# Sketched attention and a feed-forward block in one kernel: key-value matrices through DRAM instead of TensorE, and a new order of the work

## The chip, the cores and the metric

The kernel runs on one core of a Trainium2 chip. Five engines work side by side, each through its own list of instructions in order: TensorE (PE) multiplies matrices into PSUM, VectorE (DVE), ScalarE (ACT) and GpSimd (POOL) do the rest, and SyncE (SP) mostly issues transfers. Transfers can also be issued by ACT. Engines wait for each other through semaphores. The metric is the time of one execution on the device, in microseconds.

## The reference

Inputs are q, k and v of shape (4 batches, 4 heads, 1088 tokens, 32), two sketch matrices S1 and S2 of 8 x 32, and for the second block g_ln (128), w_ch1 (128 x 512) and w_ch2 (512 x 128). q, k and v are 32-bit floats; the sketches and weights arrive as 64-bit floats.

```
phi(x):   a = x @ S1.T ; b = x @ S2.T ; outer product of a and b, 64 numbers per token
kv  = sum over tokens of phi(k) (64) times v (32)
z   = sum over tokens of phi(k)
att = (phi(q) @ kv) / (phi(q) . z + 1e-6)
x   = att with the four heads side by side: (4, 1088, 128)
xn  = (x - mean) / sqrt(var + 1e-6) * g_ln
out = x + relu(xn @ w_ch1) @ w_ch2
```

## The kernel before

**Staging.** Each of the four batches has 1088 tokens. They are worked on in 9 groups u of 128 tokens (the last is a remainder). For the second block the tokens are cut into ten chunks c: chunks 0 to 7 are halves of a batch's first 1024 tokens (4 tiles of 128 each), chunks 8 and 9 hold the remainders of two batches each (one tile). All of PSUM is eight banks of 128 x 512 numbers, named A, B, C, D, M, N, O and K; the first four together are `X`, and K is also `KV`, in whose columns the key-value matrix and some small sums live.

**The order of the work** is written out in full. Every step is a small function marked `@op`; the text `PROGRAM` (L910 to L1000) lists their calls in order, with letters for the engine (V, A, G, S for DVE, ACT, POOL, SP) or the bank. Each engine runs its own steps in the order of that text. Waits follow from the data.

**The weights** (`w_ex` to `w_mul`, L275 to L342) come as 64-bit words and are turned to 32-bit floats by shifts and masks on DVE, ACT and POOL. The sketches take the same way and end in `s_heads` (L345); `sk` (L373) turns them on PE, and `sk_8`, `sk_q`, `sk_d` and others spread them into the matrices with which keys and queries are multiplied. `fold` (L359) works the mean and g_ln into the first layer's weights. `fill` and `bump` (L241 to L250) are matmuls on ones whose results nobody uses. `c_act` (L183) is a first activation; the table of functions is loaded ahead of it.

**Keys of a batch.** `turn_g` and `turn_r` (L432 to L452) turn the loaded keys on DVE, `k_feat` (L502) makes a and b on PE, `k_tok` (L514) turns them back on DVE, `k_prod` (L520) forms the 64 products, mostly on POOL. `k_sum`, `k_zs`, `k_sc` and `k_sccp` make z and merge it into the query's sketch. `k_val` (L557) sums products times values on PE into columns 0 to 63 of `KV`, each head in its own 32 partitions. Values come by `ld_v` and `ld_vr`; those of batch 0 by one load and `v_flip` and `v_cp`.

**The key-value matrix** must then stand in `kvr` turned, and spread so that each group of 32 partitions holds all heads. In the kernel before this takes three steps: `k_vcp` (L568, ACT) copies it four times side by side to `kvc`, `k_spr` (L573, PE) turns two 128 x 128 blocks into columns 256 to 511 of `KV`, `k_rcp` (L578, ACT) copies them to `kvr`.

**Queries of a batch.** `turn_h` turns them, `q_feat` (L625) makes a, b and the share of the denominator, `q_tok` (L637) turns them back, `q_ac`, `q_den`, `q_rec`, `q_a2` make the division, `q_prod` (L669) the 64 products, `q_turn` (L676) turns these on DVE. `num` (L728) multiplies them on PE with `kvr`: 32 tiles of 32 x 32, each as two matmuls, in 16 places of the array. `num_cp` and `num_r` copy the result to `xT` and `xTr`. The first 512 tokens of batch 0 go another way (`q_dir`, `q_flip`, `num0`).

**Second block.** `hid` (L841) and `relu` (L847) make one of four quarters j of the hidden layer of a chunk, `sec` (L856) the second layer of one tile of 128 tokens. The rows of x, with tokens on partitions, are wanted for the statistics (`st_bn`, `st_ag` on DVE, `st_pow` on POOL) and for the last sum. Chunks in `through_dram` (L774) get them by `row_turn` (L795, DVE), `row_wr` (L800, a write to DRAM) and four reads `row_rd` (L806); the others, here 0, 8 and 9, by `row_pe` and `row_cp` (L785 to L792), turned by PE and copied. The last sum is `fin` (L870, DVE, tile by tile) or `fin_a` and `fin_g` (L876 to L888, ACT then POOL, the whole chunk); `store` and `store_r` write out a quarter or a remainder.

```
    def k_spr(b):
        for i in range(2):
            pe.transpose(KV[:, 256 + P * i : 256 + P * (i + 1)], kvc[:, P * i : P * (i + 1)], ident)
```

Of the kernel before, what the change touches and what calls it, by code (L numbers as in the profile page):

```python
# [24 lines left out]
def kernel(  # L25
# [49 lines left out]
    def copy(eng, o, i):  # L75
        if eng == "A":
            act.copy(o, i)
# [493 lines left out]

    @op
    def k_spr(b):  # L573
        for i in range(2):
            pe.transpose(KV[:, 256 + P * i : 256 + P * (i + 1)], kvc[:, P * i : P * (i + 1)], ident)
# [460 lines left out]
```

## Time and profile before

| what | value |
|---|---|
| three runs | 104.55, 103.06, 103.91 us; median 103.91 |
| the profiled execution | 102.81 us |
| its span, first to last instruction | 100.9 us |
| mean granted PE clock | 0.998 |
| PE, DVE, POOL, ACT busy | 95.3, 74.0, 58.4, 41.3 us |
| transfers issued by SP, by ACT (calls in PROGRAM) | 81, 27 |

A profile is of one execution; its own time is that of the table's second row, and the span leaves out some time around it. In rows of groups, the numbers behind the bar are the busy time in all and the mean in ns of one, and behind a second bar how long the engine stood idle before, and for whom. Rows of the chain and of the timeline begin with the start and the length in microseconds. "PEld" are weight loads of PE, which run beside its matmuls. "SPq" and "ACTq" are the queues in which these engines issue transfers. A line number can be that of a helper: L77, L79 and L82 are the copy and the product that many steps use.

### The profile page before, as it was taken

The numbers are of one execution on the slowest core, as the hardware profiler recorded it, in microseconds if no ns is written. First come the engines' busy times: TensorE is split into PE (matmuls) and PEld (weight loads), VectorE is DVE, ScalarE is ACT, GpSimd is POOL, SyncE is SP. The second block draws the span as 40 slices with busy tenths as digits, with TensorE's granted clock in tenths as the row PEclk, the third lists the DMA queues.
The fourth block names the chain that finished last, engine by engine and source line by source line (L and its number), as shares of the span: only waits on it lengthen the run. The fifth ranks groups of instructions, "written<-read, shape, count | busy, mean of one in ns | idle before, by whom it ended". The sixth has DMA issues, their size and how long they took to land.

```text
span 100.9 us, 3433 instructions
## 1 busy us (share of the span) xinstructions
PE 95.3 (94%) x1355; PEld 68.7 (68%) x1355; DVE 74.0 (73%) x239; ACT 41.3 (41%) x119; POOL 58.4 (58%) x83
## 2 busy tenths in 40 slices
PE   5988999999999999999999999999999999999960
PEld 5765668656656779656588669854469758959950
DVE  2878989789999599699089549999559079661630
ACT  2863754979700720755513353029640030253000
POOL 7115998999588926912999189809920540057000
PEclk9999999999999999999999999999999999999999
DMA  2989999893008760030023220346146445054242
GB/s 76 272 293 389 353 370 275 272 218 88 3 6 301 212 164 3 6 130 0 6 107 106 47 59 0 109 153 187 55 107 204 143 122 148 1 115 132 77 119 64
DMA packets 12367, 13.85 MB, mean 137 GB/s; under 512 B 2880, under 2 KB 8768, under 8 KB 12352
## 3 DMA queue, kind: packets, MB, share of 16 engines
q1 hardware_dynamic: 9968, 11.67, 38.8%
...
## 4 chain that ended last, share of the span: by engine, by line
PE 78%; DMA 5%; POOL 5%; DVE 2%; ACT 2%; SPq 2%; issue 1%; ACTq 0%; POOLq 0%
PE bankO L859 8%; PE bankM L859 8%; DMA w_raw<-in_moe_w_ch_dram 5%; PE bankN L843 5%; PE bankK L560 5%; PE bankC L843 4%; PE bankK L843 4%; PE bankK L859 4%; PE bankB L843 3%; PE bankA L843 3%; PE bankD L843 3%; PE bankM L250 3%; PE bankA L859 3%; PE bankN L859 3%; POOL ob L888 2%; PE bankA L735 2%
## 5 line engine op out<-in xcount | busy, mean ns | idle before, releaser
L82 POOL TENSOR_TENSOR kp<-kf 128x1024 f32<-128x1024 f32 (+4 forms) x9 | 15.9, 1779 | 0.1
L827 POOL TENSOR_SCALAR va<-mv 128x4 f32<-128x4 f32 (+1 forms) x10 | 2.3, 228 | 18.2 <-DVE mv L822 17.7
L82 POOL TENSOR_TENSOR qp<-a,fq 128x1280 f32<-128x1280 f32 (+1 forms) x5 | 11.1, 2219 | 0.2
L859 PEld LDWEIGHTS bankO<-w,hT 128*128 128x128 f32 x80 | 9.7, 192 | 1.9 <-issue 1.9
L829 POOL TENSOR_TENSOR rstd<-va,mhalf 128x4 f32<-128x4 f32 (+1 forms) x10 | 10.3, 1034 | 0.8
L859 PE MATMUL bankO<-w,hT 128*128 128x128 f32 x80 | 10.4, 277 | 0.0
L859 PEld LDWEIGHTS bankM<-w,hT 128*128 128x128 f32 x72 | 9.0, 192 | 1.9 <-issue 1.9
L677 DVE STREAM_TRANSPOSE qpT<-qp 128x1280 f32<-128x1280 f32 (+1 forms) x7 | 9.6, 1365 | 0.0
L250 PE MATMUL bankM<-ones 128*128 128x256 f32 (+1 forms) x28 | 8.3, 440 | 1.2 <-DVE top L180 1.2
L859 PE MATMUL bankM<-w,hT 128*128 128x128 f32 x72 | 9.3, 275 | 0.0
L816 DVE BATCH_NORM_STATS2 st<-x 128x6 f32<-128x128 f32 x32 | 6.7, 272 | 2.5 <-issue 2.5
L250 PEld LDWEIGHTS bankM<-ones 128*128 128x128 f32 x28 | 5.7, 241 | 2.5 <-DVE top L180 1.2
L851 ACT ACTIVATE hT<-bankC 128x512 f32<-128x512 f32 (+1 forms) x6 | 3.3, 551 | 8.3 <-PE bankB L859 4.7
L843 PE MATMUL bankC<-xT,w 128*128 128x512 f32 x12 | 6.1, 592 | 0.0
L843 PE MATMUL bankN<-xT,w 128*128 128x512 f32 (+1 forms) x14 | 6.1, 516 | 0.0
L851 ACT ACTIVATE hT<-bankN 128x256 f32<-128x256 f32 (+1 forms) x6 | 3.0, 498 | 7.2 <-PE bankN L843 7.2
L82 POOL TENSOR_TENSOR a<-fq,rden 128x160 f32<-128x160 f32 (+1 forms) x6 | 2.8, 463 | 5.2 <-DVE rden L659 4.8
L560 PEld LDWEIGHTS bankK<-kp,vn 128*32 128x32 f32 x288 | 4.2, 110 | 2.3 <-issue 1.1
L851 ACT ACTIVATE hT<-bankK 128x512 f32<-128x512 f32 (+1 forms) x6 | 3.1, 522 | 6.2 <-PE bankK L843 5.3
L457 DVE STREAM_TRANSPOSE qT<-qn 128x512 f32<-128x512 f32 x8 | 5.5, 687 | 0.0
L843 PE MATMUL bankK<-xT,w 128*128 128x512 f32 (+1 forms) x12 | 5.4, 530 | 0.0
L735 PE MATMUL bankD<-qpT,kvr 32*32 32x288 f32 (+1 forms) x64 | 5.2, 386 | 0.0
...
## 6 DMA issues: line engine op xcount, KB each, us to landing
...
xd<-xh SPq DMA_DIRECT2D x5, 256.0 KB, 2.6
x<-xd SPq DMA_DIRECT2D x20, 64.0 KB, 2.0
out_dram<-ob SPq DMA_DIRECT2D x19, 64.0 KB, 1.7
out_dram<-ob ACTq DMA_DIRECT2D x13, 64.0 KB, 1.9
w_raw<-in_moe_w_ch_dram SPq DMA_DIRECT2D x2, 256.0 KB, 4.0
```

Source lines behind the costliest of these rows:

```text
L82: by[eng].tensor_tensor(out=o, in0=a, in1=b, op=ALU.mult)
L250: pe.matmul(M[0][:, 0:w], ones[:, 0:P], ones[:, 0:w], start=True, stop=True)
L457: dve.transpose(_ap(dst[b % 2], 0, P, P * 4 * half, [[32, 4], [P, 4], [1, 32]]), src[b][:, 512 * half : 512 * half + 512],)
L560: pe.matmul(KV[D * h : D * h + D, 0:F], vn[b][:, TW * h + D * u : TW * h + D * (u + 1)], kp[:, H * F * u + F * h : H * F * u + F * (h + 1) ...
L677: dve.transpose(_ap(qpT, 0, P, 32 * u0, [[32, u1 - u0], [TW, 8], [1, 32]]), qp[:, H * F * u0 : H * F * u1])
L735: pe.matmul(X[r][D * h : D * h + D, o : o + w], kvr[b % 2][rows, DM * f + D * h : DM * f + D * h + D], qpT[rows, c : c + w], start=(f == 0 ...
L816: dve.bn_stats(out=sts[slot(c)][:, 6 * t : 6 * t + 6], in_=row_ap(c, t))
L827: pool.tensor_scalar(out=vas[slot(c)][:, 0:n], in0=_ap(mvs[slot(c)], 0, P, 1, [[2, n]]), scalar1=1e-6, scalar2=None, op0=ALU.add)
L829: pool.tensor_tensor(out=rstds[slot(c)][:, 0:n], in0=vas[slot(c)][:, 0:n], in1=mhalf[:, 0:n], op=ALU.pow)
L843: pe.matmul(banks[z][:, 0:n], w1[:, P * j : P * (j + 1)], cols(c)[:, a : a + n], start=True, stop=True)
L851: act.activation(o, i, AF.Relu)
L859: pe.matmul(banks[z][:, DM * t : DM * (t + 1)], h[:, 512 * j + P * t : 512 * j + P * (t + 1)], w2[:, DM * j : DM * (j + 1)], start=(j == 0 ...
```

## The change

The turned and spread `kvr` is no longer made by PE and ACT. DVE turns the 64 columns of `KV` in blocks of 32 into `kvt` (`kv_turn`), one transfer writes `kvt` to DRAM (`kv_wr`), four reads put it into each group of 32 partitions of `kvr` (`kv_rd`). The layout of `kvr` is now by head, and `num` reads it so; its two inner loops change places. All ten chunks take their rows through DRAM, so `row_pe` and `row_cp` are not called any more. The whole `PROGRAM` is in another order, with other engines for some steps; SP issues 136 transfers and ACT 7. There are 17 instead of 14 `fill` matmuls. Of the new order the diff shows the start up to the numerator of the first tokens of batch 0, the stretch around `num 1`, and the tail from `row_wr S 4` on.

```diff
--- before.py
+++ after.py
@@ -478,7 +478,8 @@
     kf = const([P, NU * KW], F32, "kf", 2)
     kp = const([P, NU * H * F], F32, "kp")
     zT = const([P, HR], F32, "zT")
-    kvc = const([P, 2 * P], F32, "kvc")
+    kvt = const([P, F], F32, "kvt", 2)
+    kvx = [dram.tile([P, F], F32, name=f"xdk{i}") for i in range(B)]
     kvr = const([P, 2 * DM], F32, "kvr", 2)
 
     @op
@@ -565,20 +566,19 @@
                 )
 
     @op
-    def k_vcp(eng, b):
-        copy(eng, _ap(kvc, 0, P, 0, [[P, 2], [32, 4], [1, 32]]),
-             _ap(KV, 0, P, 0, [[32, 2], [0, 4], [1, 32]]))
-
-    @op
-    def k_spr(b):
-        for i in range(2):
-            pe.transpose(KV[:, 256 + P * i : 256 + P * (i + 1)], kvc[:, P * i : P * (i + 1)], ident)
-
-    @op
-    def k_rcp(eng, b):
-        copy(eng, kvr[b % 2], KV[:, 256:512])
-
-
+    def kv_turn(b):
+        dve.transpose(kvt[b % 2], KV[:, 0:F])
+
+    @op
+    def kv_wr(eng, b):
+        by[eng].dma_start(out=bass.AP(kvx[b].tensor, kvx[b].offset, [[F, P], [1, F]]), in_=kvt[b % 2])
+
+    @op
+    def kv_rd(eng, b, r):
+        by[eng].dma_start(
+            out=_ap(kvr[b % 2], 32 * r, 32, 0, [[F, H], [1, F]]),
+            in_=bass.AP(kvx[b].tensor, kvx[b].offset, [[F, 32], [32 * F, H], [1, F]]),
+        )
 
     QW = H * 32
     W0 = H * 3 * R
@@ -728,13 +728,13 @@
     def num(b, u0, u1):
         w = 32 * (u1 - u0)
         for f in range(2):
-            for r in range(4):
-                for h in range(H):
+            for h in range(H):
+                for r in range(4):
                     rows, o = slice(32 * r, 32 * r + 32), 32 * u0
                     c = TW * (2 * h + f) + 32 * u0
                     pe.matmul(
                         X[r][D * h : D * h + D, o : o + w],
-                        kvr[b % 2][rows, DM * f + D * h : DM * f + D * h + D],
+                        kvr[b % 2][rows, F * h + D * f : F * h + D * f + D],
                         qpT[rows, c : c + w],
                         start=(f == 0), stop=(f == 1), tile_position=(32 * r, D * h),
                     )
@@ -771,7 +771,7 @@
     rstds = const([P, 4], F32, "rstd", 3)
     hT = const([P, JC * 512], F32, "hT", 2)
     obs = const([P, 512], F32, "ob", 4)
-    through_dram = set((1, 2, 3, 4, 5, 6, 7, ))
+    through_dram = set((0, 1, 2, 3, 4, 5, 6, 7, 8, 9))
 
     def rows_of(c):
         return x[c % 4] if c < 8 else x[c - 4]
@@ -908,96 +908,99 @@
 
 
     PROGRAM = """
-    ld_w S 1 2 4; c_ones; ld_g A; c_small; c_ac 0; ld_s A 0; ld_s S 1; c_vpad 0; c_kvb; c_vpad 1;
-    fill 1 128; ld S k 0 0 16; c_act; c_pads 1; c_pads 0; fill 4 256; c_iota; ld S k 0 16 34;
-    c_ac 1; c_m2; c_ident; ld_w S 1 0 2; c_m32; c_m8; ld S k 1 0 34; ld S q 0 16 34;
-    w_low A 1 256 512; w_ex V 0 0 32; w_bits V 0 0 32; w_bits V 1 256 512; w_exf A 0 0 32;
-    ld_h S q 0 0; w_mant V 1 256 512; w_mant A 0 0 32; w_ex V 1 256 512; ld S v 0 0 32;
-    w_e2 V 0 0 32; w_addlow V 0 0 32; w_exf A 1 256 512; w_e3 V 0 0 32; turn_g k 0 0 2;
-    ld_vr S 0 1; s_heads G; fill 1 128; w_e2 A 1 256 512; fill 1 128; c_cg V; ld_vr S 0 0; bump 12;
-    turn_g k 0 2 4; ld_w S 2 0 4; sk; bump 24; sk_8 A; w_e3 V 1 256 512; sk_q; turn_r k 0;
-    ...
+    ld_w S 1 0 2; c_ones; c_small; c_vpad 0; ld_s S 0; fill 1 256; c_act; ld_s A 1; c_ac 0;
+    c_pads 0; c_pads 1; ld S k 0 16 34; c_vpad 1; c_rest; ld S k 0 0 16; fill 1 256; c_ac 1;
+    ld_w S 1 2 4; c_iota; c_ident; ld_vr S 0 0; fill 1 256; w_bits V 0 0 32; c_m8; ld_g S;
+    w_mant A 0 0 32; w_ex V 1 0 256; ld_h S q 0 0; w_ex V 0 0 32; w_bits V 1 0 256; w_exf A 0 0 32;
+    fill 1 256; w_addlow V 0 0 32; ld S q 0 16 34; c_m2; w_e2 A 0 0 32; w_exf V 1 0 256;
+    ld S k 1 0 34; w_e2 A 1 0 256; w_e3 V 0 0 32; turn_g k 0 2 4; ld S v 0 0 32; s_heads G;
+    fill 1 256; fill 1 256; turn_r k 0; w_mant V 1 0 256; w_low A 1 0 256; w_e3 V 1 0 256; sk;
+    ld S k 2 0 34; turn_g k 0 0 2; bump 24; sk_8 A; w_add V 1 0 256; k_feat 0 0 9; ld_vr S 0 1;
+    w_low A 1 256 512; w_ex V 1 256 512; c_m32; w_exf V 1 256 512; ld S q 1 0 34; sk_b;
+    w_bits V 1 256 512; bump 12; k_tok 0 0 0 9; ld_w S 2 0 4; sk_2 A; fill 1 128; k_tok 0 1 0 9;
+    fill 1 256; w_e2 A 1 256 512; turn_h q 0 0; k_prod G 0 6 9; k_sum 0; fill 1 128; k_zs 0;
+    fill 1 128; turn_r q 0; turn_h q 0 1; k_sc 0; fill 4 256; sk_q; w_mant A 1 256 512; k_sccp V 0;
+    k_prod G 0 5 6; sk_d; k_sccp F 0; w_e3 V 1 256 512; c_kvb; sk_qq 0; turn_g k 1 0 4;
+    k_prod G 0 3 5; q_feat 0 4 9; q_dir 0 4 N; k_prod G 0 0 3; q_tok 0 2 4 9; q_tok 0 0 4 9;
+    q_tok 0 3 4 9; q_tok 0 1 4 9; v_flip 0 O; q_cp A 0 4 N 16 24; v_flip 1 K; turn_r k 1;
+    fill 1 128; c_cg V; q_ac G 0 4 9; q_ac0 0 4 N 0; v_cp A 0 O; v_flip 2 D; fill 1 128;
+    v_cp A 1 K; q_den 0 0 4; v_flip 3 M; w_add G 1 256 512; v_cp A 2 D; k_feat 1 0 9; q_den 0 4 9;
+    q_rec 0 0 4; v_cp A 3 M; q_rec 0 4 9; w_mul G 1 0 256; q_b0 0 4 N 0; k_val 0; k_tok 1 0 0 9;
+    c_vpad 3; q_prod0 2 4 N 0; w_mul G 1 256 512; fold D 0 256; kv_turn 0; sk_qq 2; k_tok 1 1 0 9;
+    q_a2 G 0 4 9; kv_wr S 0; f_vcp A; q_flip 2 4 0 A; q_prod0 0 2 N 0; q_flip 2 4 1 O;
+    q_prod G 0 4 9; ld_v S 1 2; k_sum 1; q_flcp A 2 4 1 O; f_spr C; ld_v S 1 3; turn_r q 1;
+    fold M 256 512; q_flcp A 2 4 0 A; k_zs 1; turn_h q 1 1; f_rcp A C; ld_vr S 1 1; q_flip 0 2 0 A;
+    q_flip 0 2 1 M; kv_rd S 0 3; turn_h q 1 0; q_flcp A 0 2 0 A; k_sc 1; num0 2 4 O;
+    ...
+    q_a2 G 1 0 4; k_val 1; num_cp A 0 2 4 8; num_cp V 0 0 4 8; relu A M 0 2 0 2; num_cp V 0 3 4 8;
+    num_cp A 0 1 4 8; row_turn 0; relu A N 0 3 0 2; w_e2 A 2 0 512; hid C 1 3 0 4; w_add V 2 0 512;
+    row_wr S 0; ld_vr S 2 0; k_zs 2; turn_r k 3; hid D 1 2 0 4; ld_v S 2 1; num_r A 0;
+    relu A O 0 1 0 2; w_e3 V 2 0 512; relu A C 1 3 0 4; hid O 1 1 0 4; kv_turn 1; relu A D 1 2 0 4;
+    w_mul G 2 0 512; q_den 1 4 9; kv_wr S 1; turn_g k 3 0 4; hid M 1 0 0 4; ld S q 3 0 34;
+    ld_v S 2 0; q_rec 1 4 9; k_sc 2; k_feat 3 0 9; turn_h q 2 0; relu A M 1 0 0 4; q_a2 G 1 4 9;
+    relu A O 1 1 0 4; c_vpad 2; turn_r q 2; sec M 0 0; q_prod G 1 4 9; turn_h q 2 1; kv_rd S 1 2;
+    ld_v S 2 2; row_turn 1; sec M 0 2; kv_rd S 1 1; k_tok 3 1 0 9; kv_rd S 1 3; k_tok 3 0 0 9;
+    sec N 1 2; ld_vr S 2 1; k_sccp V 2; q_prod V 1 0 4; ld_vr S 3 1; k_prod G 2 0 5; q_feat 2 0 9;
+    kv_rd S 1 0; row_wr S 1; k_sum 3; q_tok 2 3 0 9; ld_v S 2 3; sec N 1 0; q_tok 2 0 0 9;
+    ld_v S 3 1; q_turn 4 9; sec M 0 3; row_rd S 0 1; ld_vr S 3 0; sec N 1 1; k_prod G 2 5 9;
+    q_tok 2 2 0 9; row_rd S 1 2; q_tok 2 1 0 9; sec M 0 1; row_rd S 1 3; k_zs 3; q_turn 0 4;
+    row_rd S 1 0; sec N 1 3; row_rd S 1 1; q_ac G 2 4 9; q_ac V 2 0 4; k_sc 3; q_den 2 0 4;
+    num 1 0 9; q_den 2 4 9; q_rec 2 0 4; q_rec 2 4 9; k_val 2; num_cp A 1 1 0 4; num_cp V 1 3 4 8;
+    num_cp A 1 2 0 4; num_cp V 1 0 0 4; num_cp A 1 1 4 8; num_cp A 1 2 4 8; num_cp V 1 0 4 8;
+    num_cp A 1 3 0 4; row_turn 2; hid B 3 3 0 4; k_prod G 3 0 5; turn_h q 3 1; row_wr S 2;
+    ...
+    sec K 3 0; q_prod V 3 0 4; row_wr S 4; kv_rd S 3 3; hid M 8 2 0 1; row_rd S 8 2; hid A 4 3 0 4;
+    relu V M 8 2 0 1; row_rd S 3 0; st_bn 2; row_rd S 8 0; hid M 8 3 0 1; relu A A 4 3 0 4;
+    hid C 8 0 0 1; q_a2 V 3 4 9; row_rd S 3 3; hid N 4 1 0 4; row_turn 5; relu A C 8 0 0 1;
+    relu A M 8 3 0 1; kv_rd S 3 0; st_ag 2; sec M 8 0; store S 0 3 0 4; relu V N 4 1 0 4; st_pow 2;
+    row_rd S 4 2; q_turn 0 4; hid C 4 2 0 4; row_rd S 4 0; kv_rd S 3 1; q_prod G 3 4 9; fin_a O 2;
+    hid D 5 3 0 4; store S 0 0 0 4; st_bn 3; kv_rd S 3 2; hid B 5 0 0 4; store S 1 1 0 4;
+    relu A D 5 3 0 4; row_rd S 8 1; hid O 4 0 0 4; store S 0 2 0 4; relu A B 5 0 0 4; q_turn 4 9;
+    row_rd S 4 3; relu A C 4 2 0 4; hid D 5 2 0 4; row_wr S 5; relu A O 4 0 0 4; row_rd S 8 3;
+    hid N 5 1 0 4; relu A D 5 2 0 4; store S 1 0 0 4; st_ag 3; st_pow 3; sec M 4 3;
+    relu A N 5 1 0 4; num 3 0 9; fin_g G 2; fin_a K 3; row_rd S 5 3; store S 1 2 0 4; row_rd S 5 2;
+    fin_g G 3; sec M 5 1; store S 1 3 0 4; num_cp A 3 0 4 8; num_cp V 3 1 0 4; num_cp V 3 2 4 8;
+    store S 2 3 0 4; num_cp A 3 1 4 8; num_cp V 3 3 4 8; num_cp A 3 2 0 4; st_bn 8; sec K 5 2;
+    store S 0 1 0 4; num_cp A 3 3 0 4; num_cp A 3 0 0 4; st_ag 8; row_turn 7; num_r A 3;
+    row_rd S 5 1; st_pow 8; hid O 7 2 0 4; row_rd S 4 1; row_turn 6; store S 2 1 0 4; row_turn 9;
+    fin M 8 0; sec K 4 0; row_wr S 7; store S 2 2 0 4; sec B 5 0; store S 2 0 0 4; row_wr S 9;
+    st_bn 4; sec B 5 3; row_wr S 6; store S 3 1 0 4; st_ag 4; sec B 4 1; row_rd S 7 0; st_pow 4;
+    row_rd S 5 0; hid N 9 1 0 1; row_rd S 7 2; hid A 9 0 0 1; hid M 9 2 0 1; store S 3 2 0 4;
+    hid D 7 3 0 4; fin K 4 0; row_rd S 6 1; store_r S 8 0; hid C 7 0 0 4; relu A D 7 3 0 4;
+    row_rd S 7 1; relu A O 7 2 0 4; store_r S 8 1; hid D 7 1 0 4; row_rd S 9 3; sec B 4 2;
+    row_rd S 9 0; relu A D 7 1 0 4; row_rd S 7 3; relu A C 7 0 0 4; hid K 9 3 0 1; row_rd S 6 0;
+    fin B 4 2; hid D 6 1 0 4; st_bn 5; row_rd S 6 3; hid C 6 0 0 4; fin M 4 3; relu A D 6 1 0 4;
+    fin B 4 1; store S 4 1 0 4; hid D 6 2 0 4; relu V C 6 0 0 4; row_rd S 9 1; row_rd S 6 2;
+    st_ag 5; hid O 6 3 0 4; st_bn 7; row_rd S 9 2; st_pow 5; store S 3 0 0 4; sec C 7 3;
+    relu A O 6 3 0 4; relu A D 6 2 0 4; sec N 7 2; fin K 5 2; fin M 5 1; fin B 5 3; fin B 5 0;
+    sec O 7 1; st_ag 7; store S 5 2 0 4; st_bn 9; st_pow 7; st_bn 6; store S 3 3 0 4; sec N 6 1;
+    store S 5 3 0 4; st_ag 6; store S 5 1 0 4; sec B 6 0; st_pow 6; store S 4 0 0 4;
+    store S 4 2 0 4; sec C 7 0; relu V A 9 0 0 1; store S 4 3 0 4; fin O 7 1; fin N 7 2; sec A 6 3;
+    fin C 7 3; fin C 7 0; relu V K 9 3 0 1; store S 7 2 0 4; store A 7 1 0 4; sec C 6 2; fin N 6 1;
+    relu A M 9 2 0 1; st_ag 9; store S 5 0 0 4; fin B 6 0; relu A N 9 1 0 1; store A 7 0 0 4;
+    st_pow 9; fin A 6 3; store A 7 3 0 4; sec D 9 0; fin C 6 2; store S 6 3 0 4; store A 6 2 0 4;
+    fill 1 256; store A 6 1 0 4; store S 6 0 0 4; fin D 9 0; store_r A 9 1; store_r S 9 0;
     """
```

More of the change, by code (lines that the diff above doesn't have):

```diff
@@ new lines @@
+    hid B 2 0 0 4; kv_turn 2; relu A O 2 2 0 4; kv_wr S 2; num_r A 1; row_rd S 0 0; q_a2 G 2 4 9;
+    hid O 2 1 0 4; row_turn 8; q_a2 G 2 0 4; ld_v S 3 3; q_prod G 2 0 4; ld_v S 3 2; hid D 2 3 0 4;
+    relu A O 2 1 0 4; relu A B 2 0 0 4; kv_rd S 2 2; hid O 3 0 0 4; relu V D 2 3 0 4; ld_v S 3 0;
+    kv_rd S 2 1; hid B 3 1 0 4; q_prod G 2 4 9; q_turn 0 4; relu A O 3 0 0 4; kv_rd S 2 0;
+    row_rd S 2 2; sec O 2 2; relu A B 3 1 0 4; row_wr S 8; row_turn 3; kv_rd S 2 3; hid D 3 2 0 4;
+    st_bn 1; row_rd S 2 3; sk_qq 3; sec O 2 3; row_rd S 2 1; k_sccp V 3; relu A D 3 2 0 4; st_ag 1;
@@ new lines @@
+    st_bn 0; st_pow 1; q_feat 3 0 9; row_rd S 2 0; row_wr S 3; sec O 2 0; q_tok 3 0 0 9;
+    k_prod G 3 5 9; fin_a N 1; q_tok 3 3 0 9; sec K 3 1; q_tok 3 1 0 9; q_tok 3 2 0 9; sec K 3 3;
+    st_ag 0; q_ac V 3 4 9; st_pow 0; q_turn 4 9; hid N 8 1 0 1; k_val 3; fin_g G 1; fin_a M 0;
+    q_ac V 3 0 4; num 2 0 9; kv_turn 3; q_den 3 4 9; kv_wr S 3; q_den 3 0 4; row_rd S 3 2;
+    q_rec 3 0 4; sec K 3 2; num_cp A 2 0 0 4; num_cp V 2 3 0 4; num_cp A 2 2 0 4; q_a2 G 3 0 4;
+    num_cp V 2 3 4 8; row_rd S 3 1; num_cp A 2 0 4 8; num_cp A 2 1 0 4; q_rec 3 4 9; fin_g G 0;
```

93 lines of the change are left out of this document (11 added, 82 removed).

## The prediction

> **What bounds the kernel now.** I read the page's totals first, then the chain that ended last, then a table by stage cut at the points where TensorE (PE) starts the query features and the numerators of a batch.
>
> ```profile
> span 100.9 us, 3433 instructions
> ...
> PE 95.3 (94%) x1355; PEld 68.7 (68%) x1355; DVE 74.0 (73%) x239; ACT 41.3 (41%) x119; POOL 58.4 (58%) x83
> ...
> PE 78%; DMA 5%; POOL 5%; DVE 2%; ACT 2%; SPq 2%; issue 1%; ACTq 0%; POOLq 0%
> ```
>
> ```profile
> 12.13:21.16 9.03, 8.92 (x218) 5.78 (x225) 8.20 (x25) 5.75 (x20) 8.35 (x9) 1.00 0.99 297
> 21.16:33.82 12.66, 12.66 (x184) 8.45 (x191) 11.49 (x31) 7.13 (x20) 10.63 (x12) 1.00 0.45 125
> 33.82:58.96 25.14, 25.14 (x500) 18.31 (x508) 19.64 (x50) 9.64 (x29) 16.16 (x14) 1.00 0.26 75
> 72.12:97.40 25.28, 25.12 (x226) 20.18 (x225) 14.18 (x64) 5.41 (x14) 7.57 (x12) 1.00 0.40 110
> 97.40:100.90 3.50, 0.00 (x0) 0.00 (x0) 0.35 (x1) 0.00 (x0) 0.00 (x0) 0.92 0.37 94
> ```
>
> The columns after the stretch are its length and the busy time of PE, weight loads, DVE, ACT and POOL, then clock and DMA. From 21.16 to 97.40 PE has hardly a gap, so these 76.24 us are a queue of matmuls one behind the other. Ahead of it lies a start in which PE waits for data, behind it a tail of 3.50. So three things are to be priced: PE work removed, the start, and whether the new order leaves PE waiting.
>
> **PE work removed.** The chain gives what a group of PE instructions holds the engine.
>
> ```profile
> 20.20 0.58 PE bankO L715 x4
> 20.79 0.37 PE bankK L575 x2
> ...
> 23.78 0.44 PE bankO L787 x4
> ...
> 60.49 0.37 PE bankK L575 x2
> ...
> 75.87 0.11 PE bankN L787
> ...
> 88.53 0.86 PE bankD L843 x2
> ...
> 95.57 0.89 PE bankK L859 x8
> ```
>
> L575 is the spreading transpose, 0.37 in each of four batches (first and last shown); three of them come after 21.16: 1.11. L787 turns the rows of chunk 0 (0.44) and, one tile each, of chunks 8 and 9 (0.11, the last shown): 0.66. Hidden and second layers (0.86 and 0.89 for a whole step) are the same in number. After 21.16, then, 1.77 us of PE work goes. The list has 17 fills for 14; those that come after q_feat 0 cost 0.2 each for 128 columns and are in the start's sum below, and the one behind the last second-layer step has nothing waiting for it: 0.
>
> **Numerators.** The loops over h and r change places; the same 64 matmuls stay.
>
> ```profile
> 40.63 0.38 PE bankA L735 x4
> ...
> 42.16 1.09 PE bankO L859 x8
> ```
>
> ```profile
> 40.56 0.45 PE L735 MATMUL bankA<-qpT,kvr 32*32 32x288 f32 x4
> ...
> 40.82 0.42 PE L735 MATMUL bankA<-qpT,kvr 32*32 32x288 f32 x4
> ...
> 41.06 0.65 PE L735 MATMUL bankA<-qpT,kvr 32*32 32x288 f32 x5
> 41.31 0.47 PE L735 MATMUL bankB<-qpT,kvr 32*32 32x288 f32 x4
> ```
>
> One numerator takes 42.16 - 40.63 = 1.53. In its first half the sixteen tiles follow each other in steps of 0.25 (40.56, 40.82, 41.06); in the second half bank A starts at 41.06 and bank B only at 41.31: where a tile gets its second weights, the queue stands. The new order meets the same tile first, so I take 0. Bounds: 0.45 lost or regained in each of four numerators, -1.8 to +1.8 (at most the whole excess of 1.53 over four steps and a bit, and as much the other way).
>
> **ACT, DVE and POOL.** ACT loses eight copies, the row copies and 20 of 27 DMA issues; DVE gains four turns of 64 columns, row turns of chunks 0, 8 and 9, and some weight decoding.
>
> ```profile
> L77 ACT COPY kvc<-bankK 128x256 f32<-128x256 f32 x4 | 1.5, 373 | 3.2 <-PE bankK L560 2.0 <-PE bankK L531 1.3
> L452 DVE STREAM_TRANSPOSE kT<-kn 128x64 f32<-128x64 f32 x4 | 0.9, 219 | 0.0
> L797 DVE STREAM_TRANSPOSE xh<-xT 128x512 f32<-128x512 f32 x7 | 4.7, 688 | 0.2
> L677 DVE STREAM_TRANSPOSE qpT<-qp 128x1280 f32<-128x1280 f32 x4 | 5.9, 1475 | 0.0
> L677 DVE STREAM_TRANSPOSE qpT<-qp 128x1024 f32<-128x1024 f32 x3 | 3.7, 1218 | 0.0
> L82 DVE TENSOR_TENSOR qp<-a,fq 128x1024 f32<-128x1024 f32 x1 | 1.2, 1224 | 0.0
> L457 DVE STREAM_TRANSPOSE qT<-qn 128x512 f32<-128x512 f32 x8 | 5.5, 687 | 0.0
> L639 DVE STREAM_TRANSPOSE fq<-bankD 128x288 f32<-128x288 f32 x3 | 1.4, 456 | 0.4 <-PE bankD L629 0.4
> ```
>
> kv_turn has the size of L452: 4 x 0.22 = 0.9; the row turns are 0.69 + 2 x about 0.2. These lie beside matmuls, as DVE is busy 19.64 of 25.14 in the middle. They cost PE nothing while DVE is in time, so I laid the three engines' new lists side by side, each instruction with the duration of its own shape. The tightest place is num 1. PE comes to it from the start of k_feat 3 (33.6 by my walk) over that step, eight second-layer steps of 0.89, a query-feature step of about 0.7 and half a microsecond of sums: 42.5. DVE, free at 33.3, has two half turns (1.4), row_turn 1 (0.69), two key and four query turns out of PSUM (8 columns groups, about 2.5 by pitch), q_prod (1.22), q_turn twice (1.48 + 1.22) and small ones (0.7): about 9.2, so 42.5 too. No margin: whatever DVE runs late there, PE waits. At num 2 I find 0.4 of margin, at k_val 3 0.3, at num 3 1.5. I charge 0 and keep 1.5 (half a microsecond at each of the first three) as the bad end.
>
> **The new DRAM way of the key-value matrix.** kv_turn, then a write, then four reads, in place of copy, transpose, copy.
>
> ```profile
> xd<-xh SPq DMA_DIRECT2D x5, 256.0 KB, 2.6
> x<-xd SPq DMA_DIRECT2D x20, 64.0 KB, 2.0
> ```
>
> ```profile
> L808 SPq DMA_DIRECT2D x<-xd x20: 303/423/511, 32.0 to 84.2; - x20
> ...
> 17.30 3.52 SPq L121 DMA_DIRECT2D vn<-in_v_dram  x7
> ```
>
> 0.2 + 2.6 + four issues of 0.43 + 2.0 is 6.5 us from k_val to num if SP is free. The new list puts some twelve microseconds of PE work between k_val 1 and num 1 (eight second-layer steps, four hidden ones), and as much before num 2 and num 3: the way is covered, cost 0. If the cover were gone, a num would wait up to 6.5.
>
> SP is in order, and a read that waits for its write holds all behind it. Behind kv_rd of batch 0 stand the last values of batch 1; behind kv_wr 2 a row read of chunk 0; behind row_wr 5 the row reads and stores of the tail. SP issues 136 transfers instead of 81. At 0.43 each, the 51 from row_wr 4 to the last read of chunk 6 take 22 us and in my walk run from 62.0 to 87.3 with their waits; st_bn 6 wants that read at 90.4, and it lands at 89.0: 1.4 us of slack. So cost 0 here, with a rival below.
>
> The Trainium skill (DMA: Bandwidth & Descriptors, "Issuing engines are not separate DMA queues") holds that issuing from several engines only saves sequencer time, usually small beside the transfer. By it the move to SP costs nothing, as in my sum. The row above gives 0.43 per issue, and 51 of them fill most of that stretch, so here I do not call it small.
>
> **The start.** It changes in order most.
>
> ```profile
> 1.17 0.60 ACTq L104 DMA_DIRECT2D s_raw<-in_S_dram  x1
> 1.80 1.28 ACT L184 ACT_TABLE_LOAD   x1 [1.80 <-issue]
> ```
>
> ```profile
> 3.72 0.17 DVE L277 TENSOR_SCALAR ex<-s_raw 16x32 uint32<-16x32 uint32 x1 [0.38 <-DMA s_raw<-in_S_dram]
> ...
> 7.83 0.29 DVE L277 TENSOR_SCALAR ex<-w_raw 128x256 uint32<-128x256 uint32 x1 [0.90 <-DMA w_raw<-in_moe_w_ch_dram]
> ```
>
> c_act now stands ahead of ld_s on ACT: 0.7 + 1.28 and a short activation put the issue at 2.2 instead of 1.17, so S lands near 4.7 instead of 3.7, and DVE's third instruction waits for it with all masks and decoding behind it. Against that the wait of 0.90 at 7.83 goes, since the first half of w1 is now loaded first. Step by step k_feat 0 comes at 8.5 (7.08 before), and q_feat 0 at 13.3 (12.13): 1.2 late. From there PE has less to do before q_feat 1: the spread (0.37) goes, half of num0 (0.58, L715) is put behind q_feat 1, and some 1.2 of waits of the old order are filled, while two fills between the value flips add about 1.0. That gives q_feat 1 at 21.3, against 21.16. Bounds: 20.5 (S not late, masks ahead) and 23.2 (nothing regained).
>
> **Sum.** 21.3 + 76.24 + 0.58 (the moved half) - 1.77 = 96.3 for the end of PE, 97.40 before. The tail keeps its 3.50: a last sum on DVE, a store. Span 99.8, 1.1 less. The profiled execution took 102.81, so 101.7; its own time lies under the lowest of the three runs (103.06), and against their median of 103.91 the same step gives **102.8**, or 1.1% faster. About 2% is what a measurement of this kernel can tell from no change: below 101.83 or above 105.99.
>
> **Rivals.**
> *The numerators regain their stop.* For it: the stop is seen at every numerator and the loop order is what changes. Against: the first tile met is the same. Worth 1.8: 101.0.
>
> *SP becomes the bound of the tail (slower).*
>
> ```profile
> SPq L808 <- DMA xd<-xh: 5.7, 3, 2.7
> ```
>
> After 58 us the old SP waited 5.7 for written rows, my walk has 1.7; and seven value loads at 17.30 took 0.50 each. With 0.07 x 51 = 3.6 from the issues and half of the missing waits, 2.0, less the 1.4 of slack, PE ends 4.2 later: 107.0. It decides once the last read of chunk 6 lands 1.4 later than 89.0. Against it: ACT's 20 issues and their waits are gone, and DMA share there is 0.40.
>
> *A late start stays late*, or DVE makes PE wait at num 1 and num 2 so that the removed work is only exchanged for waits: 1.9 or 1.5 above the forecast, 104.5. For it speaks the margin of nothing; against it that DVE idles about 1.7 in front of relu D 2 3 and can catch up.
>
> *PE cools in the start.*
>
> ```profile
> 1.17 4.43 PE L250 MATMUL bankM<-ones 128*128 128x128 f32 x14 [1.17 <-DVE top L180]
> ...
> 9.26 1.06 PE bankM L250 x4
> ```
>
> The first 1408 columns of fills took 4.43, but 512 warm ones 1.06, so 2.9 for as many: the first ones run slower by 1.5. In the new order fills end near 5.7 and PE stands 1.4 before sk and 0.8 before k_feat 0. If that makes it slow again, another 1.5: 104.3. The Trainium skill (TensorE: Matmul & The Clock Gate, "Part 1: The HAM clock gate") has the clock halve after an idle window of about 3.4 us, longer than these pauses; by that rule the rival fails, so it gets little.
>
> **Chances.** Forecast 0.47 (its own range 101.8 to 103.9), numerators 0.22, SP 0.15, late start or DVE 0.11, cooling 0.05. The range: 100.9 to 105.9 leaves out part of the numerators' case and most of SP's. Faster by over 2%: 0.22 and a low edge of the forecast, 0.25; slower by over 2%: SP's 0.15 and a little of the late start, 0.17; between, 0.58.
>
> **What would show it.** k_feat 0 near 8.5 and q_feat 1 near 21.3; no PE idle after it but for some tenths at num 1; num still 1.53; k_val to num with kvr in time; PE end near 96.3 and the tail 3.5. The prediction is wrong if q_feat 1 is off by over a microsecond, if num changes its length, or if SP's row reads are what DVE's st_bn waits for.

## The result, and the profile after

The kernel after takes 104.02 us as the median of 22 runs (103.73 to 104.81). The kernel before, run between them, has 104.26 (102.78 to 105.20). The runs of before lie around 103.0 and around 104.6, and the comparison leaves out most of the upper ones as disturbed (by the two medians alone after would be 0.2% faster): the ratio is **1.0087, interval 1.0066 to 1.0108: 0.9% slower**, within the 2%. The forecast was 102.8, 1.1% faster.

The page of the kernel after, its totals and the shares of the chain that ended last:

```profile
PE 97.7 (95%) x1347; PEld 68.6 (67%) x1347; DVE 72.3 (70%) x237; ACT 39.8 (39%) x118; POOL 58.1 (56%) x82
...
PE 61%; SPq 14%; DMA 9%; DVE 7%; issue 3%; POOL 1%; ACT 1%; DVEq 0%; POOLq 0%
```

PE is still the engine that is always busy, but 14% of the chain now is SP's queue, which had 2%. The table by stage, cut as before at the query features of batches 0 and 1, the key features of batch 3, and the last numerators (columns as in the prediction):

```profile
13.12:22.24 9.12, 9.12 (x203) 5.87 (x203) 7.13 (x24) 3.60 (x12) 9.04 (x11) 1.00 0.37 120
22.24:34.47 12.23, 12.23 (x234) 7.08 (x233) 11.03 (x27) 7.19 (x22) 5.52 (x7) 1.00 0.55 172
...
74.32:99.30 24.98, 24.78 (x218) 19.37 (x218) 13.15 (x62) 6.71 (x20) 9.46 (x15) 1.00 0.51 136
99.30:103.00 3.70, 0.42 (x2) 0.01 (x1) 0.35 (x1) 0.00 (x0) 0.00 (x0) 0.83 0.42 109
```

PE has hardly a gap behind 22.24 here either. So the question is when PE gets there, and what the queue of matmuls behind it costs. The starts below are those of the first matmul in the timeline, and the end is that of the last second-layer matmul; the chain's times, which the prediction used, are up to 0.1 later. e3 to e7 are experiments, told in the next section.

| start on PE, us | before | forecast | after | e3 | e1 | e5 | e7 |
|---|---|---|---|---|---|---|---|
| k_feat 0 | 7.09 | 8.5 | 8.05 | 8.15 | 8.16 | 8.15 | 7.89 |
| q_feat 0 | 12.06 | 13.3 | 13.12 | 13.22 | 13.23 | 12.65 | 12.39 |
| q_feat 1 | 21.09 | 21.3 | 22.24 | 22.34 | 21.08 | 20.52 | 20.26 |
| num 1 | 40.56 | 42.5 | 43.84 | 43.94 | 42.69 | 42.13 | 41.82 |
| end of the last second layer | 97.36 | 96.3 | 99.28 | 98.53 | 97.44 | 96.73 | 96.41 |
| q_feat 1 to that end | 76.27 | 75.0 | 77.05 | 76.20 | 76.36 | 76.21 | 76.16 |
| span | 100.9 | 99.8 | 103.0 | 102.2 | 101.1 | 100.4 | 100.1 |

Three things are to be told apart: q_feat 1 comes 0.9 later than forecast; from there to the end PE needs 76.2 to 77.1 where 75.0 was forecast; and the profiled execution of after, the slowest of its 22, needs 0.9 more for that than e3, whose profiled execution (104.01) stands at the median of after. In that tail SP stands in the chain (start, length, piece), and the next fence has the wait of DVE that follows:

```profile
78.45 2.19 SPq L808
...
92.35 0.46 SPq L808
...
94.11 1.16 PE bankB L859 x8
```

```profile
92.15 0.87 DVE L816 BATCH_NORM_STATS2 st<-x 128x6 f32<-128x128 f32 x4 [2.54 <-DMA x<-xd]
```

SP's row reads come late: the last of chunk 6 goes out at 92.35, where the walk of the forecast was done at 87.3. The statistics of chunk 7, whose last read goes out at about 90, let DVE wait 2.54; PE's step at 94.11 waits for DVE, and the 34 second-layer steps behind q_feat 1 take 0.8 more in all, from start to start, than in e3.

### The profile page after: what moved, and what is told of

Its sections match the earlier page's. It is cut to its first block, busy times and chain, and to the rows that moved or that the text cites. A ratio compares the mean times of both kernels' runs of the same rounds, so it can differ in the third digit from the quotient of the medians.

```text
span 103.0 us, 3456 instructions
## 1 busy us (share of the span) xinstructions
PE 97.7 (95%) x1347; PEld 68.6 (67%) x1347; DVE 72.3 (70%) x237; ACT 39.8 (39%) x118; POOL 58.1 (56%) x82
## 4 chain that ended last, share of the span: by engine, by line
PE 61%; SPq 14%; DMA 9%; DVE 7%; issue 3%; POOL 1%; ACT 1%; DVEq 0%; POOLq 0%
SPq L808 9%; PE bankO L843 5%; PE bankK L561 4%; DMA x<-xd 4%; PE bankM L250 4%; PE bankO L859 4%; PE bankM L859 4%; PE bankK L859 4%; PE bankN L859 4%; SPq L893 4%; PE bankB L843 3%; PE bankD L843 3%; DMA s_raw<-in_S_dram 2%; PE bankA L507 2%; DMA xd<-xh 2%
## 5 line engine op out<-in xcount | busy, mean ns | idle before, releaser
L250 PE MATMUL bankM<-ones 128*128 128x256 f32 (+1 forms) x34 | 10.5, 453 | 1.2 <-DVE top L180 1.2
L843 PE MATMUL bankD<-xT,w 128*128 128x512 f32 x18 | 9.4, 604 | 0.0
L250 PEld LDWEIGHTS bankM<-ones 128*128 128x128 f32 x34 | 7.3, 240 | 3.1 <-DVE top L180 1.2
L843 PE MATMUL bankO<-xT,w 128*128 128x512 f32 (+1 forms) x18 | 8.6, 562 | 0.0
L851 ACT ACTIVATE hT<-bankD 128x512 f32<-128x512 f32 x8 | 4.8, 599 | 9.6 <-PE bankD L843 9.5
L851 ACT ACTIVATE hT<-bankO 128x512 f32<-128x512 f32 (+1 forms) x9 | 5.0, 551 | 4.1 <-PE bankO L843 4.1
L859 PEld LDWEIGHTS bankK<-w,hT 128*128 128x128 f32 x48 | 5.8, 192 | 0.9 <-issue 0.5
L859 PE MATMUL bankN<-w,hT 128*128 128x128 f32 x48 | 6.4, 277 | 0.0
L859 PE MATMUL bankK<-w,hT 128*128 128x128 f32 x48 | 6.3, 277 | 0.0
L859 PEld LDWEIGHTS bankN<-w,hT 128*128 128x128 f32 x48 | 5.8, 192 | 0.0
L735 PE MATMUL bankC<-qpT,kvr 32*32 32x288 f32 (+1 forms) x64 | 5.9, 386 | 0.0
L735 PE MATMUL bankB<-qpT,kvr 32*32 32x288 f32 (+1 forms) x64 | 5.8, 386 | 0.0
```

The costliest lines, as they stand in the source:

```text
L250: pe.matmul(M[0][:, 0:w], ones[:, 0:P], ones[:, 0:w], start=True, stop=True)
L735: pe.matmul(X[r][D * h : D * h + D, o : o + w], kvr[b % 2][rows, F * h + D * f : F * h + D * f + D], qpT[rows, c : c + w], start=(f == 0), ...
L843: pe.matmul(banks[z][:, 0:n], w1[:, P * j : P * (j + 1)], cols(c)[:, a : a + n], start=True, stop=True)
L851: act.activation(o, i, AF.Relu)
L859: pe.matmul(banks[z][:, DM * t : DM * (t + 1)], h[:, 512 * j + P * t : 512 * j + P * (t + 1)], w2[:, DM * j : DM * (j + 1)], start=(j == 0 ...
```

## The experiments

e1, e2 and e6 change the start; e3, e5, e8 and e10 change what SP issues; e4 and e9 turn back one part of the change each; e7 looks at a single step of PE.

**e1: the fillers between the value turns.** Both `fill 1 128` between `v_flip 0` and `v_flip 3` are taken out.

```diff
-    v_flip 1 K; turn_r k 1; fill 1 128; c_cg V;
+    v_flip 1 K; turn_r k 1; c_cg V;
...
-    v_flip 2 D; fill 1 128; v_cp A 1 K; q_den 0 0 4; v_flip 3 M;
+    v_flip 2 D; v_cp A 1 K; q_den 0 0 4; v_flip 3 M;
```

> The kernel after, less the two fillers of one 128-column matmul each that stand between the value turns (v_flip 0 to v_flip 3); nothing reads what a filler writes, so the output is whole. In the traces the four turns and the fillers between them take 1.72 + 0.84 us after and 0.67 + 0.32 us before. Theory (TensorE's own list sets q_feat 1, and the fillers and the longer turns around them are on it): q_feat 1 moves from 22.30 to 21.1-21.5 and the whole is 0.8 to 1.2 us below after. Rival (VectorE or GpSimd sets q_feat 1, the turns only wait for copies of theirs): q_feat 1 stays within 0.3 of 22.30 and the time within 0.3 us of after. Second rival (the gain is made and lost again, because SyncE's queue sets the last chunks): q_feat 1 earlier by 1, the time by less than 0.4.

103.23 us (102.82 to 103.92; ratio to before 1.0008, 0.9972 to 1.0044), 0.8 below after. The timeline of PE in after (L466 is a value turn, L250 a filler, L507 the keys of batch 1):

```profile
14.66 0.42 PE L466 MATMUL bankO<-v,ident 32*32 32x256 f32 x4
...
15.25 0.49 PE L250 MATMUL bankM<-ones 128*128 128x128 f32 x2
15.67 0.63 PE L466 MATMUL bankD<-v,ident 32*32 32x256 f32 x8
16.23 0.49 PE L250 MATMUL bankM<-ones 128*128 128x128 f32 x2
16.65 0.63 PE L466 MATMUL bankM<-v,ident 32*32 32x256 f32 x8
17.22 0.43 PE L507 MATMUL bankA<-kT,sk 64*32 64x288 f32 x1
```

and in e1:

```profile
14.77 0.42 PE L466 MATMUL bankO<-v,ident 32*32 32x256 f32 x4
...
15.41 0.43 PE L507 MATMUL bankA<-kT,sk 64*32 64x288 f32 x1
...
16.26 1.65 PE L561 MATMUL bankK<-kp,vn 128*32 128x64 f32 x72
```

and in before, where no filler stands between the turns (L506 are the keys there):

```profile
13.65 0.42 PE L466 MATMUL bankK<-v,ident 32*32 32x256 f32 x4
...
14.32 0.43 PE L506 MATMUL bankA<-kT,sk 64*32 64x288 f32 x1
```

With the fillers this stretch takes 17.22 - 14.66 = 2.56, without them 0.64, and 0.67 in before: they cost 1.9, not two times 0.2. Each filler holds PE 0.42, and a value turn behind a filler takes 0.56 to the next step, where in e1 the four of them together take 0.64. Of the 1.9 the next steps give 0.7 back as waits (k_val 0 takes 1.58 instead of 1.14), and 1.16 arrives at q_feat 1.

**e2: the filler ahead of q_feat 0 as well.**

```diff
-    k_sc 0; fill 4 256; sk_q;
+    k_sc 0; fill 1 256; sk_q;
```

> As e1, and the filler of four 256-column matmuls ahead of sk_q is cut to one; the output is whole. In the trace of after that filler takes 1.90 us, 11.21 to 13.12, while what it bridges was ready at about 12.5. Theory: q_feat 0 moves from 13.18 to 12.5-12.8, the whole another 0.3 to 0.6 us below e1. Rival (the wait is VectorE's, the filler only lies in it): within 0.2 of e1. If TensorE's granted clock falls in the start without the filler (below 0.95 in the slices to 20 us), it is slower than e1.

103.06 (102.17 to 103.54; ratio 0.9984, 0.9945 to 1.0022). In after that filler and the wait in it:

```profile
11.21 1.97 PE L250 MATMUL bankM<-ones 128*128 128x256 f32 x8
13.11 0.32 PE L629 MATMUL bankA<-qT,skq 32*32 32x160 f32 x1
```

and in e2:

```profile
11.29 0.68 PE L250 MATMUL bankM<-ones 128*128 128x256 f32 x2
12.64 0.32 PE L629 MATMUL bankA<-qT,skq 32*32 32x160 f32 x1 [0.67 <-POOL skq L425]
```

The sketch was ready at 12.6; the filler ran 0.5 past it. q_feat 1 comes 0.57 earlier than in e1, as expected, but the time falls by only 0.17: from q_feat 1 to the end PE needs 77.04, as in the profiled run of after, and SP has 5% of the chain. The granted clock stayed at 1.0 behind the first 6.7 us.

**e3: nine stores from SP to ScalarE**, all else as after.

```diff
-    row_rd S 5 3; store S 1 2 0 4; row_rd S 5 2; fin_g G 3; sec M 5 1; store S 1 3 0 4;
+    row_rd S 5 3; row_rd S 5 2; fin_g G 3; sec M 5 1;
...
-    num_r A 3; row_rd S 5 1;
+    num_r A 3; store A 0 1 0 4; store A 1 2 0 4; store A 1 3 0 4; store A 2 3 0 4;
+    store A 2 1 0 4; store A 2 2 0 4; store A 2 0 0 4; store A 3 1 0 4; store A 3 2 0 4;
+    row_rd S 5 1;
```

> The kernel after with nine stores of batches 0 to 3 issued by ScalarE behind num_r 3 and not by SyncE among the row transfers of chunks 4 to 9; the output is whole. Theory (SyncE's list of 136 issues with stalls of 1.3 to 1.8 us makes the row transfers of the tail late: row_wr 7 at 81.7, last read at 91.4): row_wr 7 goes out 3 to 5 us earlier, the 2.54 us wait of st_bn 7 goes, the sections of chunks 6 and 7 wait 0.5 to 0.9 us less, and the time is 0.5 to 0.9 us below after. Rival (VectorE's order, or ob's store in front of fin M 8 0, sets those sections): within 0.3 us of after. Second rival: nine issues of 0.43 to 0.7 us on ScalarE delay its relus, and the time rises by 0.5 or more.

104.03 (103.91 to 104.16; ratio 1.0076, 1.0041 to 1.0111): the median does not move. But the spread does: 0.25 over 11 runs where after has 1.08 over 22. The groups of DVE's statistics (busy, mean ns, idle before them and for whom), in after and in e3:

```profile
L816 DVE BATCH_NORM_STATS2 st<-x 128x6 f32<-128x128 f32 x32 | 6.9, 278 | 3.9 <-DMA x<-xd 3.6
```

```profile
PE 88%; DVE 3%; DMA 3%; ACT 1%; issue 1%; DVEq 0%
...
L816 DVE BATCH_NORM_STATS2 st<-x 128x6 f32<-128x128 f32 x32 | 6.8, 275 | 0.2 <-issue 0.2
```

DVE's waits for rows are gone, and so is SP from the chain, and from q_feat 1 to the end PE needs 76.20 instead of 77.05. So SP's lateness is real, but in the usual run of after it costs next to nothing, net of what nine issues cost ScalarE (the fastest runs of after, 103.73, lie below e3's 103.91); the slow end of the spread goes with it.

**e4: the key-value matrices back on PE and ScalarE**, everything else as after. `k_vcp`, `k_spr` and `k_rcp` are those of before; the spread of batch 3 goes to bank M. For batch 0:

```diff
-    kv_turn 0; sk_qq 2; k_tok 1 1 0 9; q_a2 G 0 4 9; kv_wr S 0;
+    k_vcp A 0; sk_qq 2; k_tok 1 1 0 9; q_a2 G 0 4 9;
...
-    num0 2 4 O; fold_cp A D 0 256;
+    num0 2 4 O; k_spr 0 K 256; fold_cp A D 0 256;
...
-    num0_cp A 2 4 O; q_flcp A 0 2 1 M; kv_rd S 0 2;
+    num0_cp A 2 4 O; k_rcp A 0 K 256; q_flcp A 0 2 1 M;
```

> The kernel after with the key-value matrices turned and spread again as before: ScalarE copies, two TensorE transposes of 128 columns for each batch, a ScalarE copy out; kv_turn, kv_wr and the kv_rd transfers are gone (20 SyncE issues fewer). The order of the numerators' loops and all rows of x stay as after. Theory (the way through DRAM is covered and is worth the TensorE work it takes away, 4 x 0.22 to 0.28 us): 0.3 to 1.1 us above after. Rival (its 20 issues on SyncE cost more than they save): 0.3 us or more below after, with row_wr 7 earlier by several us. Between: the two cancel.

105.84 (105.69 to 106.00; ratio 1.0262, 1.0206 to 1.0319), 1.8 above after: more than either expectation. From q_feat 1 to the end PE needs 76.96, 0.76 more than in e3, which is the work of three spreads (0.71 here) and a little. Another 0.84 against e3 comes ahead of q_feat 1, where I put the first spread:

```profile
22.35 0.44 PE L575 MATMUL bankK<-ident,kvc 128*128 128x128 f32 x2
```

The waits of PE in that stretch (total, times, longest) show what follows:

```profile
PE bankA L627 <- DVE skq L553: 0.4, 1, 0.4
```

So 0.4 of the 0.84 is a wait: DVE's reduction, which reads bank K, had to wait for the spread that writes bank K, and PE for DVE. That is my placing and not the old way as such. So the way through DRAM is worth about 1.4 by my estimate (1.8 less that wait), and its 20 transfers on SP cost nothing that shows.

**e5: e2 and e3 together.**

> e2 and e3 together: no fillers between the value turns, the filler ahead of q_feat 0 cut to one, nine stores on ScalarE. Theory (after itself is set by TensorE's list, and SyncE's list lies just behind it, so that it takes over once the start comes earlier: e2's sections of chunks 6 and 7 waited 0.75 us in its trace): the gains add, PE's last section ends near 96.6 and the time is 102.1 to 102.6, that is 0.5 to 0.9 us below e2 and 1.4 to 1.9 below after. Rival (SyncE's list is never on the path, e2's tail was chance): as e2, 102.9 to 103.2.

102.22 (102.15 to 102.33), 1.8 below after; ratio to before 0.9925, 0.9888 to 0.9963. The gains add: e1 and e2 gave q_feat 1 at 20.5, and with the stores off SP the tail no longer eats it.

```profile
PE 84%; DVE 5%; POOL 3%; DMA 3%; ACT 1%; issue 1%; DVEq 0%
```

**e6: e5 with two masks earlier.** In after VectorE waits for S with the masks behind it. Its timeline:

```profile
3.77 0.17 DVE L282 TENSOR_SCALAR bits<-s_raw 16x32 uint32<-16x32 uint32 x1 [2.62 <-DMA s_raw<-in_S_dram]
3.86 0.15 DVE L206 TENSOR_SCALAR bit<-row 128x4 int32<-128x4 int32 x1
...
4.19 0.29 DVE L277 TENSOR_SCALAR ex<-w_raw 128x256 uint32<-128x256 uint32 x1
...
4.79 0.15 DVE L206 TENSOR_SCALAR bit<-row 128x2 int32<-128x2 int32 x1
...
5.05 0.29 DVE L290 TENSOR_SCALAR exf<-ex 128x256 f32<-128x256 uint32 x1
```

```diff
-    fill 1 256; w_bits V 0 0 32; c_m8; ld_g S;
+    fill 1 256; c_m8; c_m2; w_bits V 0 0 32; ld_g S;
...
-    ld S q 0 16 34; c_m2; w_e2 A 0 0 32;
+    ld S q 0 16 34; w_e2 A 0 0 32;
```

> e5 with VectorE's masks c_m8 and c_m2 (1.1 us of VectorE in the trace of after, which run there behind the first instruction that waits for the load of S) ahead of that instruction; before had them there, in the idle time up to 3.7. Theory (the start is late because VectorE stands idle up to 3.77 with work behind the wait): k_feat 0 moves from 8.05-8.2 to 7.6-7.9, q_feat 1 by 0.3 to 0.5, and the time is 0.2 to 0.5 us below e5. Rival (ScalarE's chain of S and w decoding or the turns of k set k_feat 0): within 0.1 of e5.

101.94 (101.79 to 102.10), 0.28 below e5; k_feat 0 at 7.86, q_feat 1 at 20.23. From start to start the two masks hold DVE 0.33 + 0.26 = 0.6, not the 1.1 that I had written; half of it reaches the end.

**e7: e6 with one relu earlier.** In after the second hidden step into bank O behind the first numerators finds the bank just read out. Weight loads (PEld) and ScalarE in after:

```profile
31.56 0.19 PEld L843 LDWEIGHTS bankD<-xT,w 128*128 128x128 f32 x1 [0.24 <-issue]
32.41 0.30 PEld L843 LDWEIGHTS bankO<-xT,w 128*128 128x128 f32 x2 [0.67 <-ACT hT L851]
```

```profile
30.42 0.74 ACT L310 ACTIVATE exf<-exf,m 128x512 f32<-128x512 f32 x1
31.20 0.72 ACT L311 ACTIVATE ex<-exf,top 128x512 uint32<-128x512 f32 x1
...
31.97 0.40 ACT L851 ACTIVATE hT<-bankO 128x256 f32<-128x256 f32 x1
```

Two passes of weight decoding stand ahead of the relu that frees bank O at 32.37.

```diff
-    num_cp A 0 2 4 8; num_cp V 0 0 4 8;
+    relu A O 0 1 0 2; num_cp A 0 2 4 8; num_cp V 0 0 4 8;
...
-    num_r A 0; relu A O 0 1 0 2; w_e3 V 2 0 512;
+    num_r A 0; w_e3 V 2 0 512;
```

> e6 with one relu (chunk 0, bank O) put ahead of the copies of the first numerators on ScalarE, so that bank O is read out by about 28.3 and not at 32.4, right at the start of the next hidden step into it. Theory (a weight load whose bank was not free when its turn came cannot be taken ahead, and costs 0.1 us of TensorE): the first hidden step of chunk 1 into bank O takes 0.86 and not 0.97, the hits of 0.1 behind q_feat 1 fall by one or two, and the time by about 0.1 against e6, which is less than the timing can tell. Rival (the 0.1 has another cause, such as the change of bank): the step stays at 0.97.

In e7 the same weight loads:

```profile
29.64 0.19 PEld L843 LDWEIGHTS bankD<-xT,w 128*128 128x128 f32 x1 [0.24 <-issue]
30.07 0.19 PEld L843 LDWEIGHTS bankO<-xT,w 128*128 128x128 f32 x1 [0.24 <-issue]
```

They come 0.43 apart now, one matmul ahead; the hidden step takes 0.86 instead of 0.96, and each later step of PE starts 0.1 earlier against e6. The time is 101.85 (101.77 to 101.96), 0.09 below e6, at the edge of what runs can tell; the trace carries the verdict. **Ratio to before 0.9874, 0.9833 to 0.9914; 2.1% below the kernel after.**

**e8: SP's stores doubled.** Six of its stores among the last chunks are issued twice, the first of them so:

```diff
-    row_rd S 5 3; store S 1 2 0 4; row_rd S 5 2;
+    row_rd S 5 3; store S 1 2 0 4; store S 1 2 0 4; row_rd S 5 2;
```

> The kernel after with six of SyncE's stores among the last chunks issued twice (the same rows to the same place), 6 x 0.47 = 2.8 us more on SyncE before the last reads of chunks 6 and 7. Theory (SyncE's list is within about 1 us of setting the end of after): 1.5 to 2.8 us above after, the chain that ended last runs through SyncE. Rival (it has 3 us or more of slack, as the walk of the forecast without its stalls would nearly give): within 0.4 of after.

114.54 (114.10 to 114.97; ratio 1.1133, 1.1062 to 1.1204): far above both expectations, and not a test of what it was made for. What SP's queue waited for (total, times, longest), in after and in e8:

```profile
SPq L893 <- DMA out_dram<-ob: 0.8, 1, 0.8
```

```profile
SPq L893 <- DMA out_dram<-ob: 9.0, 7, 1.5
```

Each second store to the same rows waits until the first has landed, 8.2 / 6 = 1.4 on average, and everything behind it on SP waits too: 8.2 of waits and 2.8 of issues are added, and 10.5 arrive at the end. Not all of the 10.5 is SP's own: PE stood 5.4 in one wait for DVE, up to 88.38, and from 86.4 to 93.2 the granted clock was 0.5. Three hidden steps that started in it, at 88.97, 90.68 and 92.39, took 1.71, 1.71 and 1.28 instead of 0.86, 2.1 more.

**e9: the numerators' loops turned back**, in e7.

```diff
-            for h in range(H):
-                for r in range(4):
+            for r in range(4):
+                for h in range(H):
```

> e7 with the numerators' loops turned back (rows outside, heads inside, as before the change), all else as e7. Theory (the loop order is worth nothing: the numerators of batches 1 to 3 take 1.53 us to the next step in the traces of both kernels): within 0.15 of e7. Rival (with the rows outside, one bank after the other is complete, so that the copies of the numerators can begin some tenths earlier and the weight loads behind them need not wait): the numerators still take 1.53, but 0.2 to 0.6 below e7. Second rival (heads inside stops TensorE within the numerators): 0.3 or more above.

101.89 (101.69 to 102.03; ratio to before 0.9832, 0.9768 to 0.9895): the same. The chain in e9 runs from the numerator of batch 1 to the values of batch 2 (L561) in 43.23 - 41.70 = 1.53,

```profile
41.70 0.38 PE bankA L735 x4
...
43.23 1.14 PE bankK L561 x72
```

and in after in 45.44 - 43.90 = 1.54:

```profile
43.90 0.35 PE bankA L735
...
45.44 1.14 PE bankK L561 x72
```

**e10: four more transfers on SP**, this time each to a place of its own, in the kernel after.

`extra` is the transfer of `store` with a spare tile in DRAM as its end; it stands behind the stores 1 2, 1 3, 2 3 and 2 1.

```diff
-    row_rd S 5 3; store S 1 2 0 4; row_rd S 5 2;
+    row_rd S 5 3; store S 1 2 0 4; extra S 1 2 0; row_rd S 5 2;
```

> The kernel after with four more transfers of 64 KB on SyncE among the last chunks, each a copy of a store into a spare place in DRAM of its own, so that none waits for another: 4 x 0.47 = 1.9 us more on SyncE, and nothing else that e8 had (there each second store also waited until the first had landed). Theory (SyncE's list lies within some tenths of setting the end): 1.0 to 1.9 us above after. Rival (it has 1.5 us or more of slack in the usual run): within 0.4 of after.

106.35 (106.07 to 106.93; ratio 1.0273, 1.0194 to 1.0353), 2.3 above after by the medians and 1.9 by the two ratios to before: at least all of the 1.9 added. SP is at the edge in the kernel after, in its usual runs too. The chain's end in e10 runs over SP's reads and DVE's statistics, as the tail of the profiled run of after does:

```profile
93.60 0.43 SPq L808
94.08 1.67 DMA out_dram<-ob
...
95.95 0.85 DVE st L816 x4
...
97.31 1.16 PE bankA L859 x8
```

## Why the prediction was wrong

Against the forecast, the end of the last second layer in the usual run of after (e3's trace, the same up to the stores) is late by 98.53 - 96.3 = 2.2. Two steps of the sum make it: 1.0 the start, 1.2 the queue of matmuls behind it.

1. **The start, 21.3 for q_feat 1, came out at 22.24.** q_feat 0 was a little early, 13.12 for 13.3. From it to q_feat 1 PE took 9.12, where the forecast has 8.0 and before 9.02. The step that failed is "two fills between the value flips add about 1.0" beside "some 1.2 of waits of the old order are filled". The turns with their fillers take 2.56 instead of 0.67, 1.9 more and not 1.0; all other steps of that stretch together fall by 1.8, where the spread, the moved half and the filled waits were to bring 2.15. Of the 1.9, 1.16 came through; in e1 the rest turns into waits. The filler ahead of q_feat 0 has no price in the sum either, and it ran 0.5 past what it bridged (e2). That q_feat 0 came near the forecast all the same is luck, since the reason given does not hold: c_act does not hold back ld_s. ScalarE's transfer went out while its table was still being loaded,

```profile
0.72 1.28 ACT L184 ACT_TABLE_LOAD   x1 [0.72 <-PEq L1023]
1.18 0.61 ACTq L104 DMA_DIRECT2D s_raw<-in_S_dram  x1
```

   and S was there at 3.77. Against before, q_feat 0 is 1.05 late: masks behind the wait for S make 0.3 of it (e6), the filler 0.6 (e2), and 0.2 no run explains.

2. **The PE work removed, 1.77, was 1.58, and nearly all of it was exchanged for small losses.** From one step's first matmul to the next's, the three spreads behind q_feat 1 took 0.83 before, not 1.11 (the chain's 0.37 has waits in it), and the row turns 0.75. Less the moved half (0.58, as forecast), 1.0 should go; 0.07 went (76.27 to 76.20 in e3). The forecast said that PE would have no idle time behind q_feat 1 but some tenths at num 1. It has next to none in the table by stage; but the 44 hidden and 34 second-layer steps, the same matmuls in both kernels, take 0.88 more in e3 than in before, measured from start to start, and that is nearly all of the 0.93 that is missing. In e3 22 of these 78 steps take about 0.1 more than the shortest of their form, in before ten (nine of about 0.1, one of 0.4). The cause is in part shown. e7 shows it for one step: the bank is read out too late, behind other work on ScalarE, and the first weight load is not taken ahead. In e3 eight of the 22 have a weight load that waited for ScalarE in the trace, in before two of the ten. That the others have the same cause is argued from the same size of loss and not shown. In effect this is the rival in which "the removed work is only exchanged for waits", and the late start came with it; but DVE at num 1 and num 2, which that rival named, is not where it lies: the only wait of PE itself for DVE that the profile of after names behind q_feat 1 is 0.2, at 94.11.

3. **SP, charged 0 with 1.4 of slack.** In the median run it is 0 (e3), but there is no slack: 1.9 more costs 1.9 to 2.3 (e10), and the profiled run lost 0.9 to it. DVE's statistics waited 3.6 for rows there, which was named as a sign of being wrong. The rival had the place and the mechanism, but what it counted, longer issues throughout and more waits for written rows, is not what came (such waits are 0.7 in after behind 60, and an issue still takes 0.43). By the last read of chunk 6 SP was 5 late (92.35 against 87.3); two single issues of 1.79 and 2.19 in that stretch make 3.1 of it, and the rest is not told apart. And SP was what kept the start's gain from the end (e2 against e5), which the rivals did not combine. The Trainium skill (DMA: Bandwidth & Descriptors, "Issuing engines are not separate DMA queues") has the gain of a second issuing engine as only sequencer time, usually small beside the transfer. What it saves is that here too; it is not small, since e5 with nine stores on ScalarE stands 0.8 below e2.

4. **Right:** the numerators' loop order is worth nothing (1.53 in both; e9), so their rival falls. The way of kvr through DRAM is covered (e4), and num never waits for it. PE did not cool in the start: the granted clock of after is 1.0 without a break from 6.2 to 101.7; the only fall of it ahead of PE's last steps in the traces here is e8's, behind the wait of 5.4. The tail was 3.7 instead of 3.5, by two waits of DVE's queue ahead of the last sum.

5. **The base.** The forecast carried the gain of one profiled execution, 102.81, over to a median of 103.91. For the kernel after the two do not stand so far apart (e3's trace is at its median), so part of what the forecast missed in the trace, 2.2 us, does not show in the medians: 104.02 against 102.8, a miss of 1.2. That the times hide nearly half of it is luck.
